# Top-32 attention with a mixture-of-experts layer behind it: two score products a head instead of two and three, full-width mask products, and one small threshold step moved to GpSimd

## The chip, the core and the metric

One core of a Trainium2 chip runs the whole program. Its engines are TensorE (PE in the profile; PEld is its weight load), VectorE (DVE), ScalarE (ACT), GpSimd (POOL) and SyncE (SP, here only an issuer of transfers). The metric is device time in microseconds (us) of one execution; a time is the median of several runs. Smaller is better.

## The reference, cut to what matters

```python
B, H, S, D = 4, 8, 576, 64
scores = q @ k^T / 8
kth = the 32nd largest score of each row
scores = where(scores >= kth, scores, -1e9)
attn = softmax(scores)
x = (attn @ v), heads side by side          # 2304 tokens x 512
x = moe(x)          # each token to one of 8 experts, 288 a piece
out = rational(x @ w_in) @ w_out            # 512 -> 2048 -> 512
```

Only the attention is touched by the change. All inputs and outputs are float32.

## The kernel before

The program has three parts in time: the attention, the routing of the tokens to experts, and the experts with the rational layer. The attention takes two batches and two heads at a time (eight such rounds, `si`), and each round has nine units (`u`, `NJ` = 9): a unit is 128 query rows of two heads. Four units belong to one batch, one (`j` = 4 = `R`) holds the last 64 rows of both batches, four belong to the other batch. So there are 72 units. The keys of a head are 512 "main" columns and 64 "tail" columns.

A unit goes through these stages:

- `st_scores` (L673): q·k of two heads, on TensorE. Head 0 (`hh` = 0) lies on partitions 0 to 63, head 1 on 64 to 127, so their products run side by side on two halves of the array. Head 0 wants its columns as main, tail; head 1 as tail, main, so that the two tails meet in the fifth of the nine 128-column chunks of a unit. `kT` holds main, tail for both; head 1 therefore takes three products (64, 224 and 288 columns), head 0 two (288 and 288). `COLS` (L228) lists them and `TURNS` (L671) their order. Each float32 product appears in the trace as two passes, each with a weight load of its own.
- `st_evacuate` (L688): one ScalarE copy of the scores from PSUM to `sv`.
- `st_candidates` (L729): VectorE finds the largest values of seven groups of columns and narrows them; small steps waiting in a list `later` are slipped in, one after each of the 14 group scans (`fill`, L721).
- `st_window` (L763): ScalarE takes a sign (`sg`), GpSimd multiplies (`win`, L774); VectorE's scan of `win` (L775) is put into `later`. For the last unit of a group of three (`GB` = 3), `shift` (two GpSimd steps, L757 and L758) and the threshold steps follow.
- `threshold_steps` (L783): six small VectorE steps on all six heads of a group: `rank` (L792), `equal` (L795), two products (L802: `eqt`, `eqp`) and two sums (L807: the threshold `tau`, and `pn`, a value just below it with the sign turned).
- `st_weights` (L819): ScalarE takes the sign of `sv` plus `pn` (L830), GpSimd makes the mask `mk` of it (L831).
- `st_transpose` (L834): per 128-column chunk a TensorE transpose (L841) and a product of the mask with a diagonal (L845) that adds to it. The fifth chunk holds the tails of two heads with two diagonals: there the mask product is two products of 64 columns each, on the two column halves of the array (128*64 in the trace).
- `st_spill` (L851): exponential on ScalarE; `st_av` (L860): the product with v on TensorE, 20 passes.

The order of all this is written out by hand in `step` (L1025): evacuate unit `u`, scores of `u`+1, a piece of the next round's preparation (four transposes into the score bank, then ScalarE copies in `place`, L649), spill, transpose and AV of older units, candidates of `u`, window of the unit before, weights of an older unit. Every engine runs its own queue in this order. The last stages of the last units are ordered by a small planner (`finish_attention`, L1094) with costs by engine.

Units from 66 on are groups of their own (`SG`, L697). `region` holds q transposed, and k transposed for every second round; the other rounds' k lies in a tile `kT` (L556 to L558).

Of the kernel before, what the change touches and what calls it, by code (L numbers as in the profile page):

```python
# [8 lines left out]
F32 = mybir.dt.float32  # L9
# [175 lines left out]
def kernel(  # L185
# [43 lines left out]
        [(0, 0, 0, HS), (1, 0, HS, HS)],  # L229
        [(0, 0, MAIN, TAIL), (0, TAIL, 0, HS - TAIL), (1, 0, HS - TAIL, HS)],  # L230
# [244 lines left out]
    with ExitStack() as actx:  # L475
# [62 lines left out]
        with ExitStack() as sctx:  # L538
# [18 lines left out]
            qk_raw = {nm: (carve(8 * S + 1152 * i, 2, R, 2, D), carve(8 * S + 1152 * i + 1024, 2, D)) for i, nm in enumerate("qk")}  # L557
            kT_buf = [carve(8 * S + 2304, 2 * S), lp.tile([P, 2 * S], F32, name="kT", bufs=1)]  # L558
# [15 lines left out]
            pads()  # L574

# [47 lines left out]
            def allocate(si):  # L623
                t = kT_buf[si % 2]
                prep[si] = (
                    q_T[si % 2].rearrange("p (j c) -> p j c", c=P), t.rearrange("p (b c) -> p b c", c=S)
                )
# [21 lines left out]
            def place(si, step, both=False):  # L649
                def copy(dst, src, second=False):  # L650
                    if both and second:
                        nc.vector.tensor_copy(dst, src)
                    else:
                        nc.scalar.activation(dst, src, AF.Copy)

                qT, kT = prep[si]
                ps = prep_ps.pop((si, step))
                bb = step % 2
                if step in (2, 3):
                    copy(kT[:, bb, 0:MAIN].rearrange("p (r c) -> p r c", c=P), ps, True)  # L660
                    return
                if step < 2:
                    copy(qT[:, bb * (R + 1) : bb * (R + 1) + R, :], ps)
                else:
                    copy(qT[:, R, :], ps[:, 0, :], True)
                    copy(kT[:, :, MAIN:S], ps[:, 1, :].rearrange("p (b c) -> p b c", b=2))
# [4 lines left out]
            TURNS = [(1, 0), (0, 0), (1, 1), (0, 1), (1, 2)]  # L671

            def st_scores(u):  # L673
                si, j = divmod(u, NJ)
                qT, kT = prep[si]
                sc = sc_t[u] = spare()
                for p0, n, bb in halves(j):
                    for hh, i in TURNS:
                        g, o, c, w = COLS[hh][i]
                        rows = slice(hh * D, (hh + 1) * D)  # L680
                        nc.tensor.matmul(  # L681
                            sc[p0 : p0 + n, 2 * hh + g, o : o + w],
                            qT[rows, j, p0 : p0 + n],
                            kT[rows, bb, c : c + w],
                            start=True, stop=True,
                        )
# [96 lines left out]
            def threshold_steps(t, g, tau):  # L783
# [16 lines left out]
                def pick(name, by):  # L800
                    st[name] = wk.tile([P, n, 8], F32, name=name)
                    nc.vector.scalar_tensor_tensor(  # L802
                        st[name], st["eq"], by, t["w8"][:, g], op0=OP.mult, op1=OP.mult
                    )

                def total(name, to):
                    nc.vector.tensor_reduce(to, st[name], axis=AX.X, op=OP.add)  # L807

                return [
                    rank, equal, lambda: pick("eqt", 1.0), lambda: pick("eqp", BEFORE),  # L810
                    lambda: total("eqt", tau), lambda: total("eqp", t["pn"][:, g]),
# [7 lines left out]
            def st_weights(u):  # L819
                b, i = divmod(u, GB)  # L820
                t = bat[b]
                mk = wk.tile([P, 2, S], BF16, name="mk", bufs=2)
                for hh in range(2):
                    c = 2 * i + hh
                    sv = sv_t.pop((u, hh))
                    if hh in ON_V:
                        beyond(mk[:, hh, :], sv, 2 * u + hh)
                    else:
                        sg = wk.tile([P, S], BF16, name="sg2")
                        nc.scalar.activation(sg, sv, AF.Sign, bias=t["pn"][:, c : c + 1])  # L830
                        nc.gpsimd.tensor_scalar(mk[:, hh, :], sg, -0.5, 0.5 + EPS, op0=OP.mult, op1=OP.add)  # L831
                mk_t[u] = mk.rearrange("p h s -> p (h s)")

            def st_transpose(u):  # L834
                pt = ps_t.tile([P, 3, 4, P], F32, name="pt")
                pr = pr_t.pop(u)
                mk = mk_t.get(u)
                b, i = divmod(u, GB)
                for c in range(NC):
                    o = c * P  # L840
                    nc.tensor.transpose(pt[:, c // 4, c % 4, :], pr[:, o : o + P], ident)  # L841
                    if mk is None:
                        continue
                    for p0, n, hh in [(0, P, c // (R + 1))] if c != R else [(0, TAIL, 0), (TAIL, TAIL, 1)]:
                        nc.tensor.matmul(  # L845
                            pt[p0 : p0 + n, c // 4, c % 4, :], mk[:, o + p0 : o + p0 + n],
                            bat[b]["dg"][:, 2 * i + hh, :], start=False, stop=True, skip_group_check=True,
# [246 lines left out]
            def finish_attention():  # L1094
# [51 lines left out]
                def add_weights_of(u, deps):  # L1146
                    end = [largest_of[u]] if u in largest_of else []
                    mk = {}

                    def chosen_of(hh):  # L1150
                        if not mk:
                            mk[0] = wk.tile([P, 2, S], BF16, name="mk", bufs=2)
                            mk_t[u] = mk[0].rearrange("p h s -> p (h s)")
                        beyond(mk[0][:, hh, :], sv_t.pop((u, hh)), 2 * u + hh)
# [1232 lines left out]
```

## Time and profile before

| what | value |
|---|---|
| median of 3 runs | 1241.24 us (1241.02 to 1245.92) |
| the profiled execution, its own time | 1241.38 us |
| its span, first to last instruction | 1239.6 us |
| PE busy | 1130.0 us, 91% |
| DVE busy | 1061.9 us, 86% |
| ACT busy | 1019.4 us, 82% |
| POOL busy | 375.0 us, 30% |

The page gives each engine's busy time over the span; "mean ns" of a row is the length of one instruction, which is longer than the distance between two starts where instructions overlap in the engine's pipeline. A number in square brackets behind a row is idle time of that engine just before it and what ended it. The granted TensorE clock (PEclk) is a share of full speed.

### The profile page before, as it was taken

Reading aid. Unit: us, or ns where it says so; the run is one execution under the profiler, and the core shown is the slowest. Engines: PE = TensorE matmul, PEld = TensorE weight load, DVE = VectorE, ACT = ScalarE, POOL = GpSimd, SP = SyncE. Lnnn points to the kernel's source line nnn. Section 1 sums busy time; section 2 is a strip of 40 time slices with the busy share of each in tenths; the row PEclk is TensorE's granted clock in tenths of the full one; section 3 lists DMA queues with packets and bytes.
Section 4 is the critical chain, followed back from the end, with each engine's and each line's share of the span. In section 5 each row is a group of like instructions: output and inputs, shape, how many; then the busy total and the mean of one; then the engine's idle time right before and its main releaser. Section 6 shows DMA issues by size and latency. Waiting matters only on the chain.

```text
span 1239.6 us, 27194 instructions
## 1 busy us (share of the span) xinstructions
PE 1130.0 (91%) x9879; PEld 915.3 (74%) x9879; DVE 1061.9 (86%) x4148; ACT 1019.4 (82%) x1802; POOL 375.0 (30%) x458
## 2 busy tenths in 40 slices
PE   5899999999999985884837999999999999999996
PEld 3688888888888863653625877888888888888784
DVE  6999999989898955885988979898989889897795
ACT  4899999989998985677999978888888788876684
POOL 4788777768677700001010001000101000001010
PEclk9899999999999996555868999999999999999998
DMA  5204112021100304611323222222122222100000
GB/s 124 51 10 152 41 28 50 11 50 34 27 2 2 137 2 178 234 52 55 122 88 106 99 88 88 88 82 75 32 76 88 88 74 62 41 1 21 1 20 20
DMA packets 81108, 80.63 MB, mean 65 GB/s; under 512 B 59968, under 2 KB 59968, under 8 KB 80960
## 3 DMA queue, kind: packets, MB, share of 16 engines
q1 hardware_dynamic: 77888, 69.27, 17.7%
q0 software_dynamic: 3072, 9.48, 2.6%
q8 instruction: 82, 1.34, 0.4%
q14 instruction: 66, 0.54, 0.1%
HBM read 69.25 MB, written 9.47 MB: 64 GB/s over the span
## 4 chain that ended last, share of the span: by engine, by line
PE 26%; issue 15%; ACT 7%; DVE 4%; POOL 1%; DMA 1%; POOLq 0%; DVEq 0%
PE pa L1922 3%; PE pa L1923 3%; PE pa L1924 3%; PE ph L1922 3%; PE ph L1924 3%; PE ph L1923 3%; PE po L1923 3%; PE po L1924 3%; PE po L1922 3%; ACT junk L306 2%; POOL out_dram L2308 1%; ACT w1s L1395 1%; PE pa L2297 0%; ACT wout L383 0%; DVE w2s L1400 0%
## 5 line engine op out<-in xcount | busy, mean ns | idle before, releaser
L774 POOL TENSOR_TENSOR win<-sv,sg 128x576 f32<-128x576 f32 x142 | 179.3, 1284 | 103.4 <-ACT sg L769 91.4
L738 DVE MAX8 cd<-sv 128x8 f32<-128x82 f32 (+1 forms) x1008 | 183.2, 230 | 11.2 <-ACT sv L691 8.7
L1922 PE MATMUL ph<-x,win 128*128 128x288 f16 x512 | 148.8, 291 | 10.5 <-DVE uv L2191 10.5
L873 PE MATMUL po<-vm,pT 128*128 128x65 f32 (+1 forms) x1280 | 150.5, 265 | 2.1 <-DVE x L893 1.5
L1923 PE MATMUL po<-g,wout 128*128 128x288 f16 x512 | 146.7, 287 | 2.4 <-DVE g L1913 2.4
L1924 PE MATMUL ph<-x,win 128*128 128x288 f16 x512 | 148.8, 291 | 0.0
L1923 PE MATMUL ph<-x,win 128*128 128x288 f16 x512 | 148.7, 290 | 0.0
L1922 PE MATMUL po<-g,wout 128*128 128x288 f16 x512 | 146.7, 287 | 0.9 <-ACT g L1912 0.8
L1924 PE MATMUL po<-g,wout 128*128 128x288 f16 x512 | 146.7, 286 | 0.0
L873 PEld LDWEIGHTS po<-vm,pT 128*128 128x128 f32 (+1 forms) x1280 | 138.6, 181 | 4.9 <-issue 2.1
L841 PE MATMUL pt<-ident,sv 128*128 128x128 f32 x648 | 132.0, 287 | 0.0
L845 PE MATMUL pt<-dg,mk 128*128 128x128 bf16 (+1 forms) x720 | 123.9, 225 | 0.0
L2308 POOL DMA_INDIRECT out_dram<-ob,tok x24 | 24.9, 1037 | 319.5 <-ACT ob L2304 267.5
L830 ACT ACTIVATE sg<-sv,pn 128x576 bf16<-128x576 f32 x136 | 97.8, 770 | 28.1 <-DVE pn L807 28.1
L1899 POOL DMA_INDIRECT xe<-xrows,rows_i x24 | 25.3, 1056 | 295.1 <-PE pa L1934 272.1
L769 ACT ACTIVATE sg<-sv,cut_all 128x576 bf16<-128x576 f32 x142 | 108.7, 774 | 6.2 <-DVE cut_all L744 6.1
L2182 ACT ACTIVATE z<-ph,inv 128x288 f32<-128x288 f32 x128 | 63.9, 499 | 58.7 <-PE ph L1924 57.9
L841 PEld LDWEIGHTS pt<-ident,sv 128*128 128x128 f32 x648 | 91.7, 141 | 20.8 <-issue 5.0
L775 DVE MAX8 w<-win 128x8 f32<-128x576 f32 x142 | 105.4, 743 | 0.0
L831 POOL TENSOR_SCALAR mk<-sg 128x576 bf16<-128x576 bf16 x136 | 89.5, 675 | 6.2 <-ACT sg L830 5.6
L855 ACT ACTIVATE pT<-pt 128x1152 f32<-128x1152 f32 x72 | 81.3, 1129 | 4.3 <-PE pt L845 4.0
L691 ACT ACTIVATE sv<-s 128x1152 f32<-128x1152 f32 x72 | 80.5, 1118 | 3.9 <-PE s L681 3.1
(362 smaller groups left out, 3333.2 us busy)
## 6 DMA issues: line engine op xcount, KB each, us to landing
region<-in_moe_w_dram SPq DMA_DIRECT2D x16, 2048.0 KB, 7.7
xrows<-x SPq DMA_DIRECT2D x1, 4644.0 KB
region<-in_q_dram SPq DMA_DIRECT2D x32, 128.0 KB, 2.6
region<-in_k_dram SPq DMA_DIRECT2D x32, 128.0 KB, 2.9
vm<-in_v_dram SPq DMA_DIRECT2D x32, 128.0 KB, 3.2
wout<-in_moe_w_in_dram SPq DMA_DIRECT2D x8, 511.8 KB, 8.0
region<-in_moe_w_out_dram SPq DMA_DIRECT2D x8, 511.8 KB, 3.5
win<-in_moe_w_in_dram SPq DMA_DIRECT2D x6, 511.8 KB, 7.8
```

Source lines behind the costliest of these rows:

```text
L738: nc.vector.max(cd[:, g, :], sv[:, o : o + n])
L769: nc.scalar.activation(sg, sv_t[u, hh], AF.Sign, bias=cut_all[:, 2 * u + hh, 7:8], scale=-OVER, accum_out=t["sum"][:, c : c + 1],)
L774: nc.gpsimd.tensor_tensor(win, sv_t[u, hh], sg, op=OP.mult)
L775: later.append(lambda c=c, win=win: nc.vector.max(t["w8"][:, c, :], win))
L830: nc.scalar.activation(sg, sv, AF.Sign, bias=t["pn"][:, c : c + 1])
L831: nc.gpsimd.tensor_scalar(mk[:, hh, :], sg, -0.5, 0.5 + EPS, op0=OP.mult, op1=OP.add)
L841: nc.tensor.transpose(pt[:, c // 4, c % 4, :], pr[:, o : o + P], ident)
L845: nc.tensor.matmul(pt[p0 : p0 + n, c // 4, c % 4, :], mk[:, o + p0 : o + p0 + n], bat[b]["dg"][:, 2 * i + hh, :], start=False, stop=True, ...
L873: nc.tensor.matmul(po[p0 : p0 + n, i, hh, :], sb[:, hh * (R + 1) + c, p0 : p0 + n], vm[:, bb, hh, c, :], start=(c == 0), stop=False,)
L1922: nc.tensor.matmul(acc, ah, bh, start=first, stop=False)
L1923: nc.tensor.matmul(acc, ah, bl, start=False, stop=False)
L1924: nc.tensor.matmul(acc, al, bh, start=False, stop=last)
```

## The change

Keys: `kT` becomes 640 columns wide with room for a tail on both sides of the main columns. Head 0's tail is stored behind, head 1's in front, by two ScalarE copies of 64 partitions in place of one of 128. Each head then reads its 576 columns as one run, in two products of 288. Both `kT` buffers now lie in `region`.

Masks: two fixed buffers with 64 columns of zeros between the two heads' masks, set once at the start by GpSimd. In the fifth chunk the two mask products are now 128 columns wide each, the first from the tail of head 0 and the zeros, the second from the zeros and the tail of head 1, and both add into the whole chunk.

Threshold: one product (a tensor_tensor in place of a scalar_tensor_tensor) and one sum on VectorE give `tau`; `pn` is made of `tau` by one GpSimd step `below`. It is the last of the five steps in `later`. The planner's own threshold steps, for the units that the loop leaves open, are of another form and stay as they are.

```diff
     COLS = [
-        [(0, 0, 0, HS), (1, 0, HS, HS)],
-        [(0, 0, MAIN, TAIL), (0, TAIL, 0, HS - TAIL), (1, 0, HS - TAIL, HS)],
+        [(0, TAIL, HS), (1, TAIL + HS, HS)],
+        [(0, 0, HS), (1, HS, HS)],
     ]
...
-            qk_raw = {nm: (carve(8 * S + 1152 * i, 2, R, 2, D), carve(8 * S + 1152 * i + 1024, 2, D)) for i, nm in enumerate("qk")}
-            kT_buf = [carve(8 * S + 2304, 2 * S), lp.tile([P, 2 * S], F32, name="kT", bufs=1)]
+            KW = S + TAIL
+            kT_buf = [carve(4 * S + 2 * KW * i, 2 * KW) for i in range(2)]
+            QK0 = 4 * S + 4 * KW
+            qk_raw = {nm: (carve(QK0 + 1152 * i, 2, R, 2, D), carve(QK0 + 1152 * i + 1024, 2, D)) for i, nm in enumerate("qk")}
...
+            mk_buf = [wk.tile([P, 2 * S + TAIL], BF16, name=f"mk{i}", bufs=1) for i in range(2)]
+            for m in mk_buf:
+                nc.gpsimd.memset(m[:, S : S + TAIL], 0.0)
+
+            def mask_of(u, hh):
+                return mk_buf[u % 2][:, hh * (S + TAIL) : hh * (S + TAIL) + S]
...
-                    copy(kT[:, bb, 0:MAIN].rearrange("p (r c) -> p r c", c=P), ps, True)
+                    copy(kT[:, bb, TAIL:S].rearrange("p (r c) -> p r c", c=P), ps, True)
...
                     copy(qT[:, R, :], ps[:, 0, :], True)
-                    copy(kT[:, :, MAIN:S], ps[:, 1, :].rearrange("p (b c) -> p b c", b=2))
+                    tail = ps[:, 1, :].rearrange("p (b c) -> p b c", b=2)
+                    copy(kT[0:D, :, S:KW], tail[0:D])
+                    copy(kT[D:P, :, 0:TAIL], tail[D:P])
...
-            TURNS = [(1, 0), (0, 0), (1, 1), (0, 1), (1, 2)]
+            TURNS = [(1, 0), (0, 0), (1, 1), (0, 1)]
...
-                        g, o, c, w = COLS[hh][i]
+                        g, c, w = COLS[hh][i]
...
-                            sc[p0 : p0 + n, 2 * hh + g, o : o + w],
+                            sc[p0 : p0 + n, 2 * hh + g, 0:w],
...
-                def pick(name, by):
-                    st[name] = wk.tile([P, n, 8], F32, name=name)
-                    nc.vector.scalar_tensor_tensor(
-                        st[name], st["eq"], by, t["w8"][:, g], op0=OP.mult, op1=OP.mult
-                    )
-
-                def total(name, to):
-                    nc.vector.tensor_reduce(to, st[name], axis=AX.X, op=OP.add)
+                def pick():
+                    st["eqt"] = wk.tile([P, n, 8], F32, name="eqt")
+                    nc.vector.tensor_tensor(st["eqt"], st["eq"], t["w8"][:, g], op=OP.mult)
+
+                def total():
+                    nc.vector.tensor_reduce(tau, st["eqt"], axis=AX.X, op=OP.add)
+
+                def below():
+                    nc.gpsimd.tensor_scalar(t["pn"][:, g], tau, BEFORE, None, op0=OP.mult)
...
-                    rank, equal, lambda: pick("eqt", 1.0), lambda: pick("eqp", BEFORE),
-                    lambda: total("eqt", tau), lambda: total("eqp", t["pn"][:, g]),
+                    rank, equal, pick, total, below,
...
-                    for p0, n, hh in [(0, P, c // (R + 1))] if c != R else [(0, TAIL, 0), (TAIL, TAIL, 1)]:
+                    for hh, o in [(c // (R + 1), c * P + (TAIL if c > R else 0))] if c != R else [(0, MAIN), (1, S)]:
                         nc.tensor.matmul(
-                            pt[p0 : p0 + n, c // 4, c % 4, :], mk[:, o + p0 : o + p0 + n],
-                            bat[b]["dg"][:, 2 * i + hh, :], start=False, stop=True, skip_group_check=True,
+                            dst, mk_buf[u % 2][:, o : o + P], bat[b]["dg"][:, 2 * i + hh, :],
+                            start=False, stop=True, skip_group_check=True,
                         )
```

`st_weights` and the planner's `add_weights_of` (L1146) write into `mask_of(u, hh)` in place of a fresh tile; nothing else of them is changed.

## Rows read from the trace of the kernel before

**Rows 1.** The page, the span in 40 slices: TensorE's granted clock

```profile
PEclk9899999999999996555868999999999999999998
```

**Rows 2.** Rounds of nine units: stretch, length, then PE, PEld, DVE, ACT, POOL busy

```profile
48.77:99.64 50.87, 50.87 (x490) 44.04 (x489) 49.47 (x304) 48.56 (x84) 41.15 (x46) 1.00 0.16 37
...
201.39:252.27 50.88, 50.88 (x490) 44.02 (x489) 48.36 (x297) 46.84 (x79) 39.37 (x43) 1.00 0.16 37
...
307.13:361.98 54.85, 54.85 (x526) 48.07 (x525) 48.42 (x300) 49.92 (x88) 39.25 (x43) 1.00 0.10 23
```

**Rows 3.** The same columns ahead of those rounds and behind them

```profile
13.90:48.77 34.87, 23.43 (x160) 17.14 (x159) 32.79 (x214) 25.72 (x47) 20.39 (x20) 0.76 0.32 70
...
416.83:475.00 58.17, 49.28 (x436) 38.76 (x434) 36.96 (x165) 40.33 (x54) 11.64 (x16) 0.98 0.20 74
```

**Rows 4.** Waits from 48.77 to 252 us: total us, times, longest us

```profile
ACT sg L830 <- DVE pn L807: 11.9, 12, 1.4
...
DVE den L891 <- PE po L877: 4.1, 10, 0.6
...
DVE cd L738 <- ACT sv L691: 1.9, 6, 0.4
```

**Rows 5.** Order of time on TensorE within one unit: start, length, instruction

```profile
201.39 1.35 PE L681 MATMUL s<-kT,region 64*128 64x64 f32 x10
202.68 0.33 PE L841 MATMUL pt<-ident,sv 128*128 128x128 f32 x1
...
203.24 0.28 PE L841 MATMUL pt<-ident,sv 128*128 128x128 f32 x1
203.35 0.22 PE L845 MATMUL pt<-dg,mk 128*128 128x128 bf16 x1
203.41 0.28 PE L841 MATMUL pt<-ident,sv 128*128 128x128 f32 x1
203.62 0.25 PE L845 MATMUL pt<-dg,mk 128*64 128x128 bf16 x2
203.80 0.33 PE L841 MATMUL pt<-ident,sv 128*128 128x128 f32 x1
```

**Rows 6.** Score passes in flight at 202.23 us, then at 202.34 us

```profile
201.91 0.72 PE L681 MATMUL s<-kT,region 64*128 64x224 f32 x4
...
201.99 0.76 PE L681 MATMUL s<-kT,region 64*128 64x288 f32 x4
```

**Rows 7.** Order of time on VectorE, scans with threshold steps between them

```profile
218.50 0.23 DVE L738 MAX8 cd<-sv 128x8 f32<-128x83 f32 x1
...
218.76 0.23 DVE L738 MAX8 cd<-sv 128x8 f32<-128x83 f32 x1
...
219.17 0.18 DVE L807 TENSOR_REDUCE pn<-eqp 128x6 f32<-128x48 f32 x1
219.27 0.96 DVE L738 MAX8 cd<-sv 128x8 f32<-128x82 f32 x6
...
221.39 0.34 DVE L744 MAX8 cut_all<-cm 128x8 f32<-128x56 f32 x2
221.87 0.25 DVE L738 MAX8 cd<-sv 128x8 f32<-128x82 f32 x1
222.04 0.74 DVE L775 MAX8 w<-win 128x8 f32<-128x576 f32 x1
```

**Rows 8.** Order of time on GpSimd and ScalarE around the same threshold

```profile
217.69 2.52 POOL L774 TENSOR_TENSOR win<-sv,sg 128x576 f32<-128x576 f32 x2
...
219.38 1.44 ACT L830 ACTIVATE sg<-sv,pn 128x576 bf16<-128x576 f32 x2 [1.08 <-DVE pn L807]
220.24 1.33 POOL L831 TENSOR_SCALAR mk<-sg 128x576 bf16<-128x576 bf16 x2
...
223.70 1.28 POOL L774 TENSOR_TENSOR win<-sv,sg 128x576 f32<-128x576 f32 x1 [2.12 <-ACT sg L769]
```

**Rows 9.** GpSimd's step on 128x6 values: count, ns min/median/max, first and last start

```profile
L757 POOL TENSOR_SCALAR top_all<-top x28: 218/238/257, 29.3 to 426.0; 128x6 f32<-128x6 f32 x22, 128x2 f32<-128x2 f32 x6
```

**Rows 10.** Order of time at the start: last tail copy, first scores

```profile
9.88 0.28 ACT L654 ACTIVATE region<-pt 128x128 f32<-128x128 f32 x1 [0.95 <-DVE region L652]
...
10.21 2.50 PE L681 MATMUL s<-region 64*128 64x64 f32 x10 [1.92 <-ACT region L654]
```

More of the change, by code (lines that the diff above doesn't have):

```diff
@@ L625, in allocate @@
                 prep[si] = (
-                    q_T[si % 2].rearrange("p (j c) -> p j c", c=P), t.rearrange("p (b c) -> p b c", c=S)
+                    q_T[si % 2].rearrange("p (j c) -> p j c", c=P), t.rearrange("p (b c) -> p b c", c=KW)
                 )
@@ L821, in st_weights @@
                 t = bat[b]
-                mk = wk.tile([P, 2, S], BF16, name="mk", bufs=2)
                 for hh in range(2):
@@ L825, in st_weights @@
                     sv = sv_t.pop((u, hh))
+                    mk = mask_of(u, hh)
                     if hh in ON_V:
-                        beyond(mk[:, hh, :], sv, 2 * u + hh)
+                        beyond(mk, sv, 2 * u + hh)
                     else:
@@ L830, in st_weights @@
                         nc.scalar.activation(sg, sv, AF.Sign, bias=t["pn"][:, c : c + 1])
-                        nc.gpsimd.tensor_scalar(mk[:, hh, :], sg, -0.5, 0.5 + EPS, op0=OP.mult, op1=OP.add)
-                mk_t[u] = mk.rearrange("p h s -> p (h s)")
+                        nc.gpsimd.tensor_scalar(mk, sg, -0.5, 0.5 + EPS, op0=OP.mult, op1=OP.add)
+                mk_t[u] = True
             def st_transpose(u):
@@ L836, in st_transpose @@
                 pr = pr_t.pop(u)
-                mk = mk_t.get(u)
                 b, i = divmod(u, GB)
                 for c in range(NC):
-                    o = c * P
-                    nc.tensor.transpose(pt[:, c // 4, c % 4, :], pr[:, o : o + P], ident)
-                    if mk is None:
+                    dst = pt[:, c // 4, c % 4, :]
+                    nc.tensor.transpose(dst, pr[:, c * P : (c + 1) * P], ident)
+                    if u not in mk_t:
                         continue
-                    for p0, n, hh in [(0, P, c // (R + 1))] if c != R else [(0, TAIL, 0), (TAIL, TAIL, 1)]:
+                    for hh, o in [(c // (R + 1), c * P + (TAIL if c > R else 0))] if c != R else [(0, MAIN), (1, S)]:
                         nc.tensor.matmul(
-                            pt[p0 : p0 + n, c // 4, c % 4, :], mk[:, o + p0 : o + p0 + n],
-                            bat[b]["dg"][:, 2 * i + hh, :], start=False, stop=True, skip_group_check=True,
+                            dst, mk_buf[u % 2][:, o : o + P], bat[b]["dg"][:, 2 * i + hh, :],
+                            start=False, stop=True, skip_group_check=True,
                         )
@@ L1147, in add_weights_of @@
                     end = [largest_of[u]] if u in largest_of else []
-                    mk = {}
                     def chosen_of(hh):
[L1151 to L1154, printed above, removed]
+                        mk_t[u] = True
+                        beyond(mask_of(u, hh), sv_t.pop((u, hh)), 2 * u + hh)
                     first = last.add("V", 0.5, lambda: chosen_of(0), deps, u)
```

## The prediction

> **What bounds the kernel now.** I read the granted clock over the span first: it is full through the attention, apart from its start, and about half in the slices of the routing behind it [rows 1]. The change touches the attention alone, so I cut that into its rounds of nine units. In every round from 48.77 us on, TensorE is busy for the whole stretch: 50.87 of 50.87, 54.85 of 54.85 [rows 2]. The reader should see how close the next engines are. In the early rounds (four of 50.87 us, of which two stand) VectorE is busy for 48.36 to 49.47 and ScalarE for 46.84 to 48.56; in the late ones (three of 54.85, one stands) TensorE has the logits to do as well, and VectorE's 48.42 leaves 6.4 us of room [rows 2]. Before 48.77 VectorE is the fullest, 32.79 of 34.87 [rows 3]; behind 416.83 nobody is, TensorE having 49.28 of 58.17 [rows 3]. So work taken from TensorE counts in full in the late rounds, and in the early ones only down to where VectorE, or the loop through it, takes over.
>
> **The mask products.** An ordinary chunk takes 0.17 us from one transpose to the next: 0.11 to the mask product and 0.06 from there to the next transpose [rows 5]. The fifth chunk takes 0.39 (203.41 to 203.80): its two 64-column products start only 0.21 after the transpose, and the next transpose 0.18 after them [rows 5]. With full-width products the chunk should be an ordinary one with one more mask product: 0.11 + 0.06 + 0.06 = 0.23, a gain of 0.16 a unit. The price of a mask product straight behind another is in no row; from below it costs nothing beyond the ordinary chunk (gain 0.22), from above a whole transpose and mask pair, 0.17 (gain 0.05). I take 0.06, because the next operation behind a mask product comes after just that. The Trainium skill's page "TensorE: Matmul & The Clock Gate", section "Back-to-back issue gap", gives some 81 ns to a weight load and a 128-column product in a sustained stream; by that the sum below would be 72 x 0.02 = 1.4 us less, an estimate from that page; here a mask product is left behind after 0.06.
>
> **The score products.** A block lasts 1.28 us, from 201.39 to the transpose at 202.68, with ten passes [rows 5]. Head 0's four passes of 288 columns end with the one begun at 202.23, at 201.91 + 0.72 = 202.63; head 1's six end at 201.99 + 0.76 = 202.75 [rows 6]. The columns are the same, so the two passes more cost 0.12. With four passes on each side both halves should end like head 0's; I take 0.11 a unit, and as bounds 0 (the halves hinder each other) and 0.17, a whole ordinary chunk. One unit in nine has its rows in two halves and twice the passes; I take 0.05 there, and the same bounds. A round then loses 9 x 0.16 + 8 x 0.11 + 0.05 = 2.37 us of TensorE: 50.87 becomes 48.5, 54.85 becomes 52.48.
>
> **VectorE's threshold.** Between two scans that have a small step between them lie 0.26 us (218.50 to 218.76); scans alone come every (0.96 - 0.23) / 5 = 0.146 [rows 7]. A small step costs 0.115, two fewer 0.23 a group, 0.70 a round of three groups. The product that stays has another form on the same operands and I cost that at nothing, since VectorE's slot is taken up by the scan beside it; were it not, it is 24 times some hundredths.
>
> **The hop to GpSimd.** `pn` now ends at 219.17 + 0.18 = 219.35 and ScalarE starts at 219.38 [rows 7, 8]. With two steps fewer the last VectorE step takes the place where `eqp` stood plus one scan, ending near 218.83; then a handover of 0.03 to 0.04, GpSimd's 0.24 for 128x6 [rows 9], another handover: near 219.15, about 0.23 earlier than now. What VectorE still has to do in the unit also ends 0.23 earlier, so the wait that closes this loop (`pn`, two signs, evacuation, next scan: cut at 221.73, next scan at 221.87, 0.15 [rows 7]) stays as it is. For the hop I keep 0.22 as the lower bound and as the upper one a queue behind both `win` products, 2.52 [rows 8]; I take 0.32, because the step stands ahead of them in program order.
>
> **What waits behind it.** GpSimd takes its steps in order, and the two `win` products of the next unit stand behind `below`. They start at 217.69 now; they would start after 219.15, end near 221.67, and the masks would end near 223.0 instead of 221.57. GpSimd then sat idle for 2.12 until 223.70 [rows 8], so 0.7 remains and the delay does not go on. Who waits: VectorE scans the first `win` at 222.04 [rows 7], when it has been done since about 220.4; the transposes of those masks are one unit later. So I cost the delay at nothing; with the cover gone it is up to 1.45 us a group.
>
> **Small things.** The second tail copy: at most 0.28 on ScalarE a round [rows 10], in rounds where ScalarE has 4 us of room, three of them the wait for `pn` (11.9 over 12 groups [rows 4]): nothing. At the start it lies on the path, since the first scores wait for the last copy [rows 10]; I add 0.15, and the first scores, which take 2.50 for ten passes there [rows 10] against 1.35 later [rows 5], give back some 0.2. Memsets of zeros at the start lie long before the first mask. No transfer is added or moved; the buffers' new places change no order.
>
> **The sum.** Until 48.77, two groups' threshold steps: -0.4. First round: VectorE needs 49.47 - 0.70, and its wait for evacuations, 1.9 over four rounds [rows 4], 0.48: 49.25, against 48.5 for TensorE; -1.6. Its waits on TensorE (4.1 [rows 4]) I let go, as TensorE comes earlier. Next three rounds: VectorE 48.36 - 0.70 + 0.48 = 48.1, TensorE 48.5; 0.1 for two engines that close together; -2.25 each, -6.8. Three late rounds -2.37 each, -7.1. Behind 416.83 six transposed units, 0.16 each, of which I count about 0.6. Together -16.5. The profiled execution took 1241.38 us, 1.8 over its span and 0.14 over the median of the runs; 1241.38 - 16.5 = 1224.9.
>
> **Rivals.**
> *The loop through VectorE, GpSimd and ScalarE takes over in the early rounds.* For it: the engines lie within 5% of each other, and a handover or GpSimd's queue may cost more than I took. Against it: GpSimd is free for about a second microsecond before `below`. If each of the twelve early groups loses 0.4, 5 us of the 8.4 go: 1230. Chance 0.20.
> *The fifth chunk is not dear for its narrow products.* Two narrow products run side by side, so widening them only adds one: -0.06 a unit, while the scores give 0.11: 72 x 0.05 = 3.6, 1237.8. For it: both narrow products start together [rows 5]; against it: nothing else explains 0.21 ahead of them and 0.18 behind. The Trainium skill's page "TensorEngine Tiling (Array Packing)", section "When to Use Tiling", gives the packing of 64-column weights up to twice the speed, which speaks against this edit; its section "Key Properties" says that changing the tiling mode drains the engine, which speaks for it. By the first the time is this rival's, by the second the forecast's; the 0.39 of the fifth chunk sides with the second. Chance 0.06.
> *`pn` comes late through GpSimd's queue: slower.* If `below` is held back behind both `win` products, it ends 2.5 us later than I reckon. A group of the early rounds has 16.96 us, VectorE needs 15.9 with its 0.15; a delay over 0.9 a group makes it slower than now. At 2.3 it loses 1.4 in each of twelve groups, and the late rounds lose their gain: 1241 + 17 = 1258. Program order speaks against it. Chance 0.05.
> *The gain is given back behind the attention.* The routing runs at half clock [rows 1], and where the clock comes back depends on what TensorE does around it; a clock that comes back 10 to 20 us later would take back some 10: 1235. For it, only that everything behind is shifted in time. Chance 0.07.
>
> **How the numbers follow.** The forecast keeps 0.62. A measurement of this kernel can tell about 0.5%, 6.2 us, from no change. Faster by more: forecast, the loop, and half of the last rival: 0.62 + 0.20 + 0.035 = 0.855. Within: the narrow products and the other half: 0.095. Slower: 0.05. The range: the bounds of the second mask product (0.06 and 0.11 a unit) and of the scores carry the forecast from 1224.9 down to 1219 at most, as VectorE stops the early rounds; upward it takes in the loop with its 1230 and some more: 1219 to 1233.
>
> **What would show it.** Transposes of a unit: 0.23 between the fifth and the sixth; score blocks of eight passes and 1.17 us; rounds of 48.6 and 52.5; ScalarE's wait for a value of GpSimd in place of `pn` from VectorE, no longer in total; `win` after `below` with no new wait of VectorE on it. It is wrong if TensorE shows idle time in the early rounds, or if the stages behind 475 us take another length.

## The result and the profile after

The changed kernel takes 1226.8 us (median of 4 runs, 1225.8 to 1227.85) beside 1241.45 us for the kernel before (4 runs): a ratio of 0.9874 (95% interval 0.9850 to 0.9898). The forecast was 1224.9 us, the range 1219 to 1233. That the time is near is in part luck: the rounds gained more than forecast and the finish less than nothing, and the two met in the sum. The profiled execution is the slowest of the four, 1227.85 us.

Read as before the forecast: the granted clock over the span first, from the page of the changed kernel.

```profile
span 1226.1 us, 26893 instructions
PEclk9899999999999975555978999999999999999998
```

Against [rows 1] the 7 in the slice from 429 to 460 us is new. In the kernel before, the clock fell at 472.5 us, 9 us ahead of the routing's first product (481.6); now it falls at 445.5, 22 us ahead of it (467.6). That comes back below. Next the stretches that answer to [rows 2, 3]: stretch, length, then busy time of PE, PEld, DVE, ACT and POOL, granted clock, DMA share, GB/s. The bounds are again the starts of a score block.

```profile
13.90:48.67 34.77, 22.37 (x144) 15.24 (x142) 32.64 (x212) 25.80 (x49) 20.61 (x21) 0.80 0.32 71
48.67:97.49 48.82, 48.15 (x469) 41.78 (x469) 47.75 (x296) 47.44 (x82) 40.37 (x46) 1.00 0.17 38
193.78:241.91 48.13, 48.01 (x470) 41.77 (x469) 47.18 (x292) 46.82 (x80) 39.95 (x46) 1.00 0.17 39
293.85:345.79 51.94, 51.94 (x506) 45.85 (x505) 47.55 (x295) 50.12 (x89) 39.95 (x46) 1.00 0.11 25
397.49:461.14 63.65, 54.77 (x443) 42.21 (x442) 39.90 (x162) 41.40 (x58) 15.01 (x22) 0.85 0.18 68
```

An early round is down from 50.88 to 48.13, a late one from 54.85 to 51.94. In the late round TensorE is still busy from end to end. In the early one it is not: 48.01 of 48.13. VectorE has 47.18 there, and its four gaps (three of 0.18 and one of 0.41, all waits for an evacuation) make 0.95; together 48.13, the whole round. So the early rounds have changed hands, though only just. The last stretch here runs from the last score block to the last transpose of the logits. [rows 3] starts it at 416.83, where no score block starts: the last one starts at 415.60, so the third late round of the kernel before took 53.6 us and not 54.85. The same stretch of the kernel before (59.4 us, and the row ends 0.2 behind it) ran at a mean clock of 0.98, where the changed kernel has 0.85:

```profile
415.60:475.20 59.60, 50.51 (x445) 39.65 (x444) 38.36 (x169) 41.56 (x58) 12.46 (x16) 0.98 0.19 72
```

TensorE in one unit, the answer to [rows 5]: start, length, instruction (x2: two in this row).

```profile
204.08 1.24 PE L692 MATMUL s<-region 64*128 64x288 f32 x8
205.25 0.33 PE L851 MATMUL pt<-ident,sv 128*128 128x128 f32 x1
...
205.98 0.28 PE L851 MATMUL pt<-ident,sv 128*128 128x128 f32 x1
206.10 0.28 PE L855 MATMUL pt<-dg,mk 128*128 128x128 bf16 x2
206.21 0.28 PE L851 MATMUL pt<-ident,sv 128*128 128x128 f32 x1
206.32 0.22 PE L855 MATMUL pt<-dg,mk 128*128 128x128 bf16 x1
...
206.89 0.95 PE L883 MATMUL po<-vm,pT 128*128 128x65 f32 x7
```

The score block takes 205.25 - 204.08 = 1.17, from 1.28. From the fifth transpose to the sixth are 0.23, from 0.39. The sixth chunk also got shorter: its mask product follows its transpose by 0.11 (206.21 to 206.32), where before it followed by 0.16 (203.80 to 203.96 in the same view of the kernel before). All nine chunks, from the first transpose to the first product with v, take 1.645 (1.857 before), so 0.21 went, not 0.16. The weight loads (PEld) show where the time before went; here those of the fifth chunk's two mask products, in the kernel before and then in the changed one:

```profile
203.62 0.11 PEld L845 LDWEIGHTS <-mk 128*64 128x64 bf16 x2
```
```profile
205.98 0.21 PEld L855 LDWEIGHTS <-mk 128*128 128x128 bf16 x2
```

The full-width weights are loaded from the moment that the chunk's transpose starts (205.98); the narrow ones only 0.21 behind its start (203.41), together with their products.

The new hop, and the waits from 48.67 to 241.9 us (total, times, longest):

```profile
211.21 0.19 DVE L816 TENSOR_REDUCE tau_all<-eqt 128x6 f32<-128x48 f32 x1
...
211.48 0.24 POOL L819 TENSOR_SCALAR pn<-tau_all 128x6 f32<-128x6 f32 x1 [0.84 <-PE pt L855]
211.68 2.52 POOL L785 TENSOR_TENSOR win<-sv,sg 128x576 f32<-128x576 f32 x2
...
211.75 1.45 ACT L841 ACTIVATE sg<-sv,pn 128x576 bf16<-128x576 f32 x2 [1.12 <-POOL pn L819]
```
```profile
ACT sg L841 <- POOL pn L819: 5.2, 8, 1.2
DVE cd L749 <- ACT sv L702: 3.9, 16, 0.4
```

From the end of VectorE's sum (211.40) to the start of ScalarE's sign (211.75) are 0.35, and the step stands ahead of both `win`, as forecast. ScalarE waits less for `pn`, 5.2 against 11.9 in [rows 4], but VectorE waits more for its scores: 3.9 against 1.9.

### The profile page after: what moved, and what is told of

The parts are those of the page before. It is cut to its first block, busy times and chain, and to the rows that moved or that the text cites. A ratio compares the mean times of both kernels' runs of the same rounds, so it can differ in the third digit from the quotient of the medians.

```text
span 1226.1 us, 26893 instructions
## 1 busy us (share of the span) xinstructions
PE 1114.8 (91%) x9719; PEld 900.6 (73%) x9719; DVE 1056.6 (86%) x4094; ACT 1021.4 (83%) x1810; POOL 381.4 (31%) x487
## 4 chain that ended last, share of the span: by engine, by line
PE 27%; issue 15%; ACT 6%; DVE 4%; POOL 1%; DMA 1%; POOLq 0%; DVEq 0%
PE pa L1929 3%; PE pa L1930 3%; PE ph L1929 3%; PE pa L1931 3%; PE ph L1930 3%; PE ph L1931 3%; PE po L1930 3%; PE po L1931 3%; PE po L1929 3%; ACT junk L306 2%; POOL out_dram L2315 1%; ACT w1s L1402 1%; PE pa L2304 0%; ACT wout L383 0%; DVE w2s L1407 0%
## 5 line engine op out<-in xcount | busy, mean ns | idle before, releaser
L749 DVE MAX8 cd<-sv 128x8 f32<-128x82 f32 (+1 forms) x1008 | 178.5, 231 | 12.0 <-ACT sv L702 11.9
L851 PE MATMUL pt<-ident,sv 128*128 128x128 f32 x648 | 126.3, 283 | 0.0
L855 PE MATMUL pt<-dg,mk 128*128 128x128 bf16 x720 | 120.5, 221 | 1.5 <-POOL mk L842 1.3
L692 PE MATMUL s<-region 64*128 64x288 f32 (+1 forms) x640 | 92.7, 438 | 16.2 <-ACT region L663 11.8
```

The costliest lines, as they stand in the source:

```text
L692: nc.tensor.matmul(sc[p0 : p0 + n, 2 * hh + g, 0:w], qT[rows, j, p0 : p0 + n], kT[rows, bb, c : c + w], start=True, stop=True,)
L749: nc.vector.max(cd[:, g, :], sv[:, o : o + n])
L851: nc.tensor.transpose(dst, pr[:, c * P : (c + 1) * P], ident)
L855: nc.tensor.matmul(dst, mk_buf[u % 2][:, o : o + P], bat[b]["dg"][:, 2 * i + hh, :], start=False, stop=True, skip_group_check=True,)
```

## The experiments

Each run had runs of the kernel before on the same chip; their medians were 1244.08, 1243.88 and 1243.68 us for the three sets of four.

**The three edits one by one.** e1 has the keys alone:

```diff
...
-            TURNS = [(1, 0), (0, 0), (1, 1), (0, 1), (1, 2)]
+            TURNS = [(1, 0), (0, 0), (1, 1), (0, 1)]
...
+                    copy(kT[0:D, :, S:KW], tail[0:D])
+                    copy(kT[D:P, :, 0:TAIL], tail[D:P])
```

> Only the keys' part: two score products a head, old mask products, old threshold steps. If TensorE's work sets the rounds and a shorter score block is passed on whole (theory): blocks of 1.17 us in place of 1.28, a round of nine units 1.03 us shorter (8 x 0.11 + 0.15), 49.85 and 53.8; seven rounds 7.2 us: 1234. If a loop through the other engines sets the early rounds (rival), only the three late rounds gain: 3.1 us, 1238. The stretch from the last round to the routing stays at 58 us by the theory that GpSimd's new step lengthened it.

e2 has the masks alone:

```diff
...
-                    for p0, n, hh in [(0, P, c // (R + 1))] if c != R else [(0, TAIL, 0), (TAIL, TAIL, 1)]:
+                    for hh, o in [(c // (R + 1), c * P + (TAIL if c > R else 0))] if c != R else [(0, MAIN), (1, S)]:
...
```

> Only the masks' part: zeros between the masks and full-width products in the fifth chunk. Theory: transposes of a unit 1.65 us in place of 1.86, a round 1.9 us shorter: 48.97 (VectorE would need 48.4 and its waits 0.5, so just not the bound) and 52.95; seven rounds 13.4, and some 0.6 behind them: 1227.5. Rival (VectorE and its loop already stop the early rounds): 49.5, four rounds lose 0.5 each: 1229.5. If the longer stretch ahead of the routing comes from TensorE being early, and not from GpSimd's new step, it shows here too: 1231.

e3 has the threshold alone:

```diff
...
-                    rank, equal, lambda: pick("eqt", 1.0), lambda: pick("eqp", BEFORE),
-                    lambda: total("eqt", tau), lambda: total("eqp", t["pn"][:, g]),
+                    rank, equal, pick, total, below,
```

> Only the threshold's part. Theory: TensorE sets the rounds, so two VectorE steps fewer and the hop to GpSimd change no round: 50.87 and 54.85 stay; ScalarE waits for the value from GpSimd no longer than before; if GpSimd's step makes the masks of the single units late, the last stretch grows by up to 2 us: 1241 to 1243. Rival (VectorE sets the early rounds): four rounds of 50.2: 1238.6.

e4 is the whole change but for the threshold, which stays with its six VectorE steps:

```diff
...
-                    rank, equal, pick, total, below,
+                    rank, equal, lambda: pick("eqt", 1.0), lambda: pick("eqp", BEFORE),
+                    lambda: total("eqt", tau), lambda: total("eqp", t["pn"][:, g]),
```

> The whole change but for the threshold, which keeps its six VectorE steps and no GpSimd step. Theory: TensorE would allow rounds of 47.9, VectorE needs 48.4 and some waits, so early rounds come out near 48.9 (0.75 longer than with the whole change, four rounds 3 us), late rounds stay at 51.9; the stretch ahead of the routing gets back the 4 us that GpSimd's step in the single units cost: 1226. Rival (the stretch is longer because TensorE is early and its clock falls): the 4 us stay and the sum is 1229.8.

Measured:

| run | us | ratio (95%) | early round | late round | last score block to routing |
|---|---|---|---|---|---|
| before | 1244.08 | 1 | 50.87 | 54.85 | 66.02 |
| e1 keys | 1236.29 | 0.9938 (0.9915 to 0.9962) | 49.83 | 53.83 | 66.57 |
| e2 masks | 1233.66 | 0.9913 (0.9894 to 0.9932) | 48.98 | 52.97 | 70.30 |
| e3 threshold | 1241.75 | 0.9986 (0.9972 to 1.0000) | 50.86 | 54.85 | 67.74 |
| e4 keys, masks | 1228.95 | 0.9861 (0.9839 to 0.9883) | 48.70 | 52.01 | 68.84 |
| all three (its own runs of before: 1241.45) | 1226.8 | 0.9874 (0.9850 to 0.9898) | 48.14 | 51.94 | 70.14 |

An early round of e1 and one of e2, in the columns of the stretches above:

```profile
198.01:247.84 49.83, 49.83 (x471) 42.08 (x470) 48.36 (x298) 46.99 (x81) 39.19 (x43) 1.00 0.17 37
```
```profile
195.78:244.76 48.98, 48.98 (x490) 43.71 (x489) 47.95 (x299) 46.50 (x80) 39.16 (x43) 1.00 0.16 37
```

In both TensorE is still busy throughout, so the round's loss is the price of the edit itself: the keys 1.04 a round, the masks 1.89, that is 0.21 a unit. e3 shows the other side: two VectorE steps fewer a group change no round as long as TensorE has 50.87 to do. e4 shows when they count: with TensorE's work cut, the six steps hold the early round at 48.70, and the threshold's edit is then worth 0.56 a round. Four such rounds are 2 us, which the times by themselves don't tell apart (0.9861 beside 0.9874).

The last column was not expected. The first theory was that `below` makes the finish longer: the last groups are of one unit, GpSimd's queue is full there, and in the changed kernel TensorE waits 1.28 us for a mask at 402.82. But e2 has no `below` on GpSimd and the same long finish, and its clock is half in two places:

```profile
402.00:410.00 8.00, 8.00 (x47) 6.56 (x47) 8.00 (x50) 4.86 (x9) 4.00 (x6) 0.57 0.28 89
420.00:427.60 7.60, 7.60 (x67) 7.03 (x67) 2.96 (x9) 5.59 (x6) 0.00 (x0) 0.55 0.01 2
```

**Is it the hop or the clock?** e5 takes the step off GpSimd for the groups of one unit:

```diff
-                    nc.gpsimd.tensor_scalar(t["pn"][:, g], tau, BEFORE, None, op0=OP.mult)
+                    engine = nc.vector if n == 2 else nc.gpsimd
+                    engine.tensor_scalar(t["pn"][:, g], tau, BEFORE, None, op0=OP.mult)
```

> The changed kernel with the lower threshold on VectorE for the groups of one unit alone, on GpSimd for all others. Theory A (the finish is 4.1 us longer because GpSimd's queue is full there and TensorE waits 1.28 us for a mask behind it): the wait goes, the stretch from the last score group to the routing falls from 70.1 to 68.5 us or less, the time from 1226.8 to about 1225.4. Theory B (the finish is longer because TensorE stands on its low clock in it, which e2 showed without any step on GpSimd): the stretch stays within 1 us of 70 as long as the half-clock slices stay, and the time within 1 us of 1226.8. Both: the rounds before keep 48.14.

Measured: 1229.43 us, ratio 0.9875 (0.9854 to 0.9895). The waits for the mask are gone, and the stretch is 73.0 us, longer still, with the clock at 0.50 from 396 to 406 us and at 0.57 from 416 to 424. Theory A falls. What else may have made it worse than the changed kernel shows in e6.

e7 asks what a later `pn` costs; it issues the same step three times:

```diff
+                    for _ in range(3):
                         nc.gpsimd.tensor_scalar(t["pn"][:, g], tau, BEFORE, None, op0=OP.mult)
```

> The changed kernel with the lower threshold issued three times over on GpSimd in place of once, so two steps of 0.22 us more, 0.44 us later for each group of units. Theory (the hop lies on VectorE's and ScalarE's slack in the late rounds, and VectorE alone sets the early ones): ScalarE's waits for pn grow by up to 0.44 us a group, and the rounds stay within 0.1 us of 48.14 and 51.94, since VectorE issues nothing more; the time within 1 us of 1226.8, but the groups of one unit at the end add up to 0.44 us each on GpSimd's full queue, some 1 to 2 us in the finish. Rival (each group's masks wait for pn, and with them TensorE): three groups a round, up to 1.3 us more a round, rounds of 48.6 to 49.5, the time up to 1236.

Measured: 1239.74 us, ratio 0.9965 (0.9947 to 0.9982); early rounds 49.98 to 50.01, late ones 53.21. The slack that the theory counted on is not there, and even the rival was too low. An early round and a late one, and the waits as above:

```profile
199.55:249.53 49.98, 48.19 (x470) 41.78 (x469) 47.16 (x292) 46.84 (x80) 41.24 (x52) 1.00 0.17 38
302.76:355.97 53.21, 52.16 (x506) 45.81 (x506) 47.67 (x295) 50.12 (x89) 41.28 (x52) 1.00 0.11 25
...
DVE cd L749 <- ACT sv L702: 12.4, 16, 1.6
ACT sg L842 <- POOL pn L820: 12.4, 12, 1.8
```

In the early round VectorE has as much to do as in the changed kernel (47.16 beside 47.18) and waits for the evacuation instead, three times 0.80 a round where the changed kernel waits three times 0.18: 1.86 us, which is the round's growth (49.98 - 48.13 = 1.85). The road is ScalarE's queue: the sign that wants `pn` stands ahead of the next unit's evacuation, and VectorE's next scan wants that. The delay was more than the 0.44 reckoned with:

```profile
218.19 0.86 POOL L820 TENSOR_SCALAR pn<-tau_all 128x6 f32<-128x6 f32 x3 [0.86 <-DVE tau_all L816]
...
219.09 1.44 ACT L842 ACTIVATE sg<-sv,pn 128x576 bf16<-128x576 f32 x2 [1.77 <-POOL pn L820]
```

The three steps end 0.86 behind the start of the first, where the one step took 0.24, so `pn` came 0.62 later and cost 0.62 a group: the early rounds have no room for a later `pn` at all. The late rounds have little: VectorE's 47.67 leaves room there, but TensorE now sits idle for 1.05 of 53.21, and the round is 1.27 longer, 0.42 a group.

e6 goes the other way and puts the step on VectorE for every group (`nc.vector` in place of `nc.gpsimd` in that line).

> The changed kernel with the lower threshold on VectorE for all groups: five small VectorE steps in place of six before and four after. Theory A (VectorE's count of steps sets the early rounds): one step of 0.115 us more for three groups, rounds of 48.4 to 48.5, time about 1228. Theory B (e7 showed that a later pn makes ScalarE evacuate the next scores later, and VectorE wait for them: 0.62 us for 0.44; in the changed kernel that wait is still 0.18 us three times a round, and it would go): 0.35 more and 0.54 less, rounds of 47.95 to 48.1, down to TensorE's own bound, time 1225.5 to 1227. Both: late rounds 51.94.

Measured: 1240.47 us, ratio 0.9974 (0.9960 to 0.9988); early rounds 49.72, late ones 53.60. Both theories fall, because the step does not take 0.115. All 27 of it (count, ns min/median/max, first and last start), then one of them beside GpSimd's product, which began before it:

```profile
L819 DVE TENSOR_SCALAR pn<-tau_all x27: 152/920/1114, 33.5 to 423.4; 128x6 f32<-128x6 f32 x22, 128x2 f32<-128x2 f32 x5
```
```profile
215.94 2.52 POOL L785 TENSOR_TENSOR win<-sv,sg 128x576 f32<-128x576 f32 x2
216.81 0.43 DVE L819 TENSOR_SCALAR pn<-tau_all 128x6 f32<-128x6 f32 x1
```

Here two `win` products stand in one row; the first ends at 217.22, the step at 217.24. In 26 of the 27 cases the step ends 0.02 to 0.03 us behind the end of a `win` product that was under way when it started, whether that end was 0.13 or 1.1 us away. VectorE does 49.29 us of work in the early round, 2.1 more than the changed kernel, and three such steps, in this round 0.92, 1.01 and 0.43, account for it. The sums that the kernel before used for the same value (L807) took 0.15 to 0.19 beside such products; [rows 7] shows one of 0.18. The Trainium skill's page "SBUF — State Buffer", section "Who interferes with whom", says that VectorE's tensor_scalar can take a pair of ports that it shares with GpSimd, that the pair is an exclusive lock for a whole instruction, and that a tensor_reduce never wants it; the rows agree in both halves. They also show that not every tensor_scalar of this size is held. `rank`, the first threshold step, is one as well, and in the kernel before it lay inside a `win` product 19 times and took 0.15 to 0.17 each time:

```profile
201.23 1.28 POOL L774 TENSOR_TENSOR win<-sv,sg 128x576 f32<-128x576 f32 x1
```
```profile
201.50 0.17 DVE L792 TENSOR_SCALAR po<-sum 128x6 f32<-128x6 f32 x1
```

`rank` writes its values to PSUM, `pn` lies in SBUF, the memory of the tiles that it is made of; `rank` also does two operations where `pn` takes one, and no run changes one of the two alone. In e5 the five moved steps took 0.17 to 1.26 us each in place of GpSimd's 0.22, which may be one reason why its finish got no better.

**The clock.** e8 was to add dummy products in the last six logits tiles, to see whether the long tail is the low clock's doing, and e9 to add them to e5:

```diff
...
+                    st = {"n": len(late_tiles)}
...
+                    def fill():
+                        for _ in range(4 if st["n"] >= 12 else 0):
+                            nc.tensor.matmul(st["ps"][:, 1, 2 * P : 3 * P], onesb, onesb, start=True, stop=True)
...
```

> The changed kernel, with dummy TensorE products added in the last six logits tiles: four of 128 columns behind a tile's transposes and four behind its second product, whose results nobody reads, so that TensorE has more to do while VectorE copies. Theory (the logits tail is longer because TensorE falls to the low clock at 446 us and its transposes and products then take 1.0 to 1.1 us in place of 0.6 to 0.66): if the clock stays up, the stretch from the last score group to the routing falls from 70.1 to 66 or 67 us and the time to about 1223.5. Rivals: the clock falls in spite of them, and they lengthen a tile by up to 0.45 us at full clock and 0.9 at half: stretch 71 to 73, the time 1228 to 1230; or the tail's length is VectorE's copies, whatever the clock: no change.

> Both of the runs before together: the lower threshold on VectorE for the groups of one unit, and the dummy products in the last six logits tiles. If both effects exist they add: the stretch falls to 65 to 66 us and the time to about 1222. If only one does, it is where that one alone stands.

Measured: e8 1223.91 us, ratio 0.9843 (0.9822 to 0.9864), no half clock in the profile between 44 and 452 us, stretch 65.9; e9 1230.04 us, 0.9878 (0.9858 to 0.9899), half clock in places from 260 us on and from 451 us to the routing, stretch 70.5.

But no dummy was ever issued. The planner adds nine logits tiles, counted from 0 to 8, and the condition asks for a count of 12. The pages of e8, of e9 and of e5:

```profile
span 1220.6 us, 26893 instructions
```
```profile
span 1231.8 us, 26898 instructions
```
```profile
span 1231.1 us, 26898 instructions
```

e8 has as many instructions as the changed kernel, and e9 as many as e5, and they are the same instructions in each group. So e8 is the changed kernel a second time, e9 is e5 a second time, and what more work for TensorE would do to the clock in the tail is not tested. What the pair does give is the changed kernel and e5's version beside each other: 1223.91 us against 1229.43 and 1230.04, though single executions overlap (1222.31 to 1227.57 against 1225.88 to 1233.5).

The changed kernel (e10), e8's once more (e11) and e6 with the same added lines (e12) then ran beside one another:

> The changed kernel itself, unaltered, on the chip of the three runs beside it: the measure for them. Theory (TensorE falls to the low clock in the logits tail of this version each time, for that tail is reached by the same steps): rounds of 48.14 and 51.94 again, stretch from the last score group to the routing 68 to 71 us with the half clock from about 446 us, time 1226 to 1228. Rival (where the clock falls is chance from execution to execution): rounds the same, but the stretch anywhere from 66 to 71 us, and other half-clock slices than at 404 and 446 us.

> The kernel of e8 once more (dummy products in the last six logits tiles), beside the changed kernel on the same chip. Theory (the dummies hold the clock through the tail): no half clock before 452 us, stretch about 66 us, time 1222 to 1225, and 2 to 4 us under e10. Rival (e8 met a good execution; e9 fell to half clock at 450 us with the same dummies): stretch 68 to 71 us, time within 1 us of e10.

> The kernel of e6 with the dummy products of e8. If the dummies hold the clock: stretch about 66 us and 2 to 4 us under e6. If they don't: within 1 us of e6. With theory B of e6 and the first of e11 both right it is the fastest of the four, 1221 to 1224.

Measured: e10 1224.39 us (1222.5 to 1227.19), ratio 0.9855 (0.9834 to 0.9876); e11 1225.99 us (1224.95 to 1226.65), 0.9860 (0.9840 to 0.9879); e12 1241.54 us, 0.9982 (0.9967 to 0.9996), beside 1240.47 for e6. e11 and e12 hold no dummy either (26893 instructions and 26920, as the changed kernel and e6), so their theories on the dummies are as untested. The rival of e10 holds: where the clock falls differs from execution to execution. The result, e8, e10 and e11 are four profiles of one program. From the last score block to the routing's first product, the kernel before, then the result, e10, e8 and e11:

```profile
415.60:481.62 66.02, 50.51 (x446) 39.68 (x446) 40.48 (x182) 43.62 (x64) 14.03 (x19) 0.93 0.19 70
```
```profile
397.49:467.64 70.15, 54.77 (x444) 42.25 (x444) 42.44 (x176) 43.61 (x65) 16.49 (x25) 0.82 0.19 66
```
```profile
396.41:462.95 66.54, 50.12 (x443) 39.59 (x443) 42.27 (x176) 43.28 (x63) 16.63 (x25) 0.93 0.20 68
```
```profile
396.60:462.46 65.86, 49.38 (x443) 39.31 (x443) 42.27 (x176) 43.29 (x63) 16.62 (x25) 0.93 0.19 68
```
```profile
399.16:465.20 66.04, 49.51 (x444) 39.33 (x443) 42.27 (x176) 43.35 (x63) 16.63 (x25) 0.93 0.19 69
```

Where the clock of this stretch is that of the kernel before, 0.93, so is its length, 65.9 to 66.5 us. The one profile at 0.82 is the one with 4 us more. The times of the single executions go the same way. Of the 17 of this program, eight had a mean clock of 0.926 to 0.928 and took 1222.3 to 1225.8 us, nine had 0.918 to 0.922 and took 1225.8 to 1227.9; all four of the result's are among the nine. Of 48 executions of the kernel before beside these runs, 12 had 0.920 to 0.922 and took 1246.2 to 1247.3 us, the others 0.924 or more and 1240.0 to 1246.4. The finish of the result's execution in parts, then that of e10, whose profiled execution spans 1220.8 us in place of 1226.1:

```profile
404.00:407.40 3.40, 3.30 (x23) 2.91 (x23) 3.40 (x31) 1.89 (x3) 3.23 (x5) 0.58 1.00 394
407.40:445.30 37.90, 34.19 (x326) 28.90 (x325) 25.56 (x79) 33.16 (x44) 6.21 (x10) 0.99 0.11 42
445.30:461.14 15.84, 11.94 (x49) 5.85 (x47) 4.42 (x17) 0.00 (x0) 0.00 (x0) 0.51 0.00 1
```
```profile
396.41:442.00 45.59, 40.84 (x391) 34.67 (x390) 34.15 (x139) 41.42 (x58) 15.14 (x22) 1.00 0.26 93
442.00:446.00 4.00, 2.85 (x13) 1.55 (x13) 1.41 (x7) 0.00 (x0) 0.00 (x0) 0.69 0.03 10
446.00:456.30 10.30, 6.21 (x41) 3.21 (x39) 4.33 (x17) 0.00 (x0) 0.00 (x0) 0.95 0.00 0
```

The same work, from the last score block to the last transpose of the logits, takes 63.65 us with the clock at half twice, and 60.11 with it at half for a part of four. In the logits tail each step waits for the one before, so TensorE's length counts there; four passes of a product in the result's execution, before and after the fall:

```profile
444.81 0.60 PE L1198 MATMUL s<-xt,wg 128*8 128x128 f32 x4 [0.92 <-DVE xt L1194]
...
448.14 1.02 PE L1198 MATMUL s<-xt,wg 128*8 128x128 f32 x4 [0.54 <-DVE xt L1194]
```

What one fall costs where TensorE sets the pace, e11 shows in two neighbouring late rounds, with equal counts of instructions on TensorE and no idle time on it in either:

```profile
241.97:293.91 51.94, 51.94 (x506) 45.85 (x505) 47.38 (x294) 49.90 (x89) 39.80 (x46) 1.00 0.16 36
293.91:347.45 53.54, 53.54 (x506) 46.68 (x505) 47.55 (x295) 50.27 (x89) 39.95 (x46) 0.97 0.11 25
```

1.60 us, for about 3.4 at half clock. e4 and e9 each have one late round that is 1.6 longer in the same way.

## Why the prediction was right, and where not

By the profiled executions (the result's, and e10's as a second one of the same kernel), each against the one of the kernel before:

| term | forecast | result | e10 |
|---|---|---|---|
| until the ninth score block (48.77) | -0.4 | -0.1 | -1.1 |
| first round | -1.6 | -2.1 | -2.1 |
| next three, together | -6.8 | -8.2 | -8.3 |
| three late ones, together | -7.1 | -7.8 | -7.8 |
| last score block to routing | -0.6 | +4.1 | +0.5 |
| routing and what follows | 0 | +0.5 | -0.2 |

**The score products: right.** 0.11 a unit was forecast and 0.11 came, and e1 confirms it by itself. The unit with its rows in two halves was taken at 0.05 and gave 0.15 (its passes went from 20 to 16, its block from 1.293 to 1.145), since it gains for each half.

**The mask products: right in kind, mis-sized.** The 0.23 from the fifth transpose to the sixth is the forecast value; a second mask product follows the first by 0.056. What the term left out is that the narrow pair also delayed the mask product of the chunk behind it, by 0.05. e2 measures 0.21 a unit for the edit where the term has 0.16. The rival of the narrow products is excluded by that run: 0.06 a unit would have been lost and 0.21 was won. The page "TensorEngine Tiling (Array Packing)" of the Trainium skill was quoted for both sides; its section "Key Properties", that a change of mode drains the engine, is the one that the trace agrees with, in that the narrow weights were loaded 0.21 behind the start of the transpose and not beside it; no run separates such a drain from another reason. The "up to twice" that the forecast quotes stands under "Theoretical Speedup" on that page; "When to Use Tiling" has the factor of two alone.

**The early rounds: the bound was named wrongly.** The forecast let TensorE set them at 48.5 and gave VectorE 48.1, and it named idle time of TensorE there as a sign of being wrong: there is some, 0.12 in the round shown. With both terms above at their measured size, TensorE would allow 50.87 - 9 x 0.212 - 8 x 0.110 - 0.148 = 47.93; the rounds came out at 48.14, by VectorE's work and its gaps. That its 48.1 came true is luck: its work is 47.18 where the forecast had 47.66, and its gaps are 0.95 where it had 0.48. The rival of the loop through VectorE, GpSimd and ScalarE had the mechanism, in a mild form: the waits for evacuations did not stay as they were (1.9) but doubled (3.9 over four rounds); e3, in which TensorE still sets the rounds, has 3.7, so it is the threshold's edit that doubles them. It costs 0.2 a round and not 0.4 a group, and e7 shows how near the edge that is.

**The hop: right.** 0.32 was taken, 0.35 came, `win` stands behind it, and no wait of VectorE on `win` appeared. That GpSimd is the right place was not argued in the forecast; e6 shows it, by 1.6 us a round.

**The finish: wrong.** The step that failed is "behind 416.83 six transposed units, of which I count about 0.6". At the clock of the kernel before, nothing of it came: 65.9 to 66.5 us beside 66.0, in a stretch in which TensorE has work for 50. In the result's execution the finish took 4.1 us more, in e10's 0.5 more, and what separates the two is the granted clock. The mask's wait of 1.28 us is not it: the profile of e8 has two such waits, 1.27 and 1.15 us, and a stretch of 65.9. The forecast let the clock come back late behind the attention as a rival, and had no term for a fall within it. So the sum had 16.5, the result's execution 13.5 and e10's 18.9 us: with the clock of the kernel before in the finish the forecast was too small, with that of the result's execution too large.

**What stays open** is why the clock falls where it does. In the profiles here it is full from 44 us to the logits tail in the kernel before, e3, e8 and e10, and falls once or more ahead of it in the others, e11 among them, which is the same program as e8 and e10. Some of these falls come behind idle time of TensorE (in the result's execution at 404.6, half a microsecond behind the end of the mask's wait, a wait that e8 has too, without a fall), some in rounds in which TensorE was never idle. Nine low executions of 17 beside 12 of 48 do not settle whether the changed kernel falls more often. No version tried beats the changed kernel beyond the spread of its own runs (1222.3 to 1227.9).

## What to carry to other kernels

Price an edit on a pipelined engine from the whole block that it stands in, first instruction to first instruction of the next, and not from the pair of rows where it shows most: the narrow pair cost time in the chunk behind it as well. When two engines lie within 2% of each other, take the work off one and look at the other's waits; here a value that was 0.62 us later cost 0.62, through a third engine's queue. Profile the same kernel twice before explaining a difference of a few microseconds by one trace of each: four profiles of one program put 65.9 to 70.1 us on the same finish. And count the instructions in the trace of an experiment before reading its time: four runs here were to hold dummy products, and none did.

## What the runs showed of the hardware that was not expected

A VectorE step on 128x6 values, 0.15 us at its shortest, took up to 1.11 us in e6 (1.26 in e5) because it ended only when GpSimd's product of two tensors ended; the same value made by a sum on VectorE (0.18) or by GpSimd itself (0.24) did not wait, nor did a step of the same kind and size that writes to PSUM (0.15 to 0.17). TensorE's granted clock fell to half in steady, gapless work, for 3.4 us in e11 (which cost 1.6), and for 10 us in e5 behind some idle time, at other places in each execution; two executions of one kernel differed by 5.3 us of span, 3.6 of it in the finish. And narrow mask products on the two column halves cost 0.21 us more than full-width products of twice the columns: 0.16 until the next transpose, 0.05 behind it.
